# Two-stage kernel (normalised linear attention, then routed experts): outputs stored per pair of tiles, the end of the attention stage reordered, one weight load held back

## The chip, the cores and the metric

The kernel runs on one core of a Trainium2 chip. The metric is the device time of one execution in microseconds. The core has TensorE (PE; PEld is its weight load), VectorE (DVE), ScalarE (ACT), GpSimd (POOL) and SyncE (SP, which only issues DMAs here). ACT, POOL and SP issue DMAs, all of which run on 16 DMA engines.

## What is computed

```python
kv = np.einsum('bhsd,bhse->bhde', k, v)          # 8 batches, 8 heads, 576 rows, 64 columns
out = np.einsum('bhsd,bhde->bhse', q, kv)
rms = np.sqrt(np.mean(out * out, axis=-1, keepdims=True) + 1e-06)
x = out / rms * g_norm                           # -> x: 4608 rows of 512
skip_score = x @ w_skip                          # rows with skip_score <= 0 stay as they are
e_idx = np.argmax(x @ w_gate, axis=1)            # one of 8 experts
gate_w = softmax(x @ w_gate)[e_idx]
h = np.maximum(x @ w1[e], 0.0)                   # 512 -> 1024
x += gate_w * (h @ w2[e])                        # 1024 -> 512, for the rows of expert e
```

All inputs and the output are float32.

## The kernel before, in words

**Attention stage.** The 4608 rows are 36 tiles of 128 rows, taken as 18 pairs. A pair is worked in two units `u`, each for four heads, so there are 36 units, n = 0 to 35. Four batches make a round: each batch has two pairs (`i` = 0, 1) of eight of its nine rows per partition, and a ninth pair (`i is None`, units 16, 17, 34, 35) takes the ninth rows of four batches. The loop at L837 writes the order out by hand. In step n it emits: PE's transposes of q for unit n+1 (`turn`), ACT's root of the sums of squares of unit n-1 (`root`), PE's products of unit n into a PSUM tile and ACT's squares of them (`values`, L466 or L474 and L480), DVE's reciprocal and scaling of unit n-1 (`norm`, L502 and L507, result `xl`), DVE's sum of squares of unit n (`squares`, L488), then PE's work on the state of a later batch, then POOL's adding up of the logits that came along as extra columns (`finish`, L524 to L532, result `lg`). From unit 28 on, three PSUM tiles rotate (two `o_ps` and `sum_ps`, which units 28, 31 and 34 use), so the products of unit n wait for `xl` of unit n-3.

POOL's multiplication by `g_norm` (L547, result `xb`) is put into a list and run one unit later, behind the next reciprocal (`scale`; the note in the code reads "VectorE's port is free then"). `xb` is a buffer for both pairs of a batch, and there are two of them; the ninth pair has one buffer of its own, `x8`. When a buffer is full, the upper 64 partitions are stored by a DMA that POOL issues and the lower 64 by one that SP issues two steps later (L576, L577; L569, L570 for `x8`). Units 34 and 35 are scaled together behind the last logits.

**Choice and ranks.** For three groups of tiles (12, 10 and 14: `ends`), `choose` (L583) turns `lg` into a one-hot choice `ohb` on DVE; `rank` (L614) counts on PE, with an upper triangle `ut` and matrices of ones, each row's place among its expert's rows, and separately the group's count per expert; `number` (L631) adds the sums so far (`top`), picks the place and makes one-hot operands `oha_k`. The first two groups run in pieces inside the loop. After the second, experts are ordered by size, and SP loads expert 0's weights (2 MB `w1`, 2 MB `w2`) into `wpool_a`. `early` places the first 128 rows of the first expert and gathers them from `out`.

**Expert stage** (L867 on). `expert_in` transposes gathered rows on PE (L973) and copies them on ACT (L976, L978); `layer_1` is L996 and L998, `layer_2` is L1007. The stage begins with expert 0's first 128 rows, and the last group is handled between its parts: `choose(LAST)`, `columns` for the first 22 tiles, five eighths of `layer_1`, `rank(LAST)`, `number(LAST)`, the rest of `layer_1`, and `settle` (L680, L743), which places the row numbers in two parts, each beside a part of `layer_2`. Then `slot_rows` and `again_rows` give the row numbers, POOL issues indirect gathers from `out` (L963), which need all stores of x done, and `load_ahead(0)` has SP load expert 1's weights. Experts 1 to 7 use a product scheme with fewer multiplications (L1075 to L1085), whose weight sums DVE makes (L1017, L1023). Results go back by indirect scatters (L1217).

The instructions of each engine stand in the order in which the code emits them; only waits are added.

Of the kernel before, what the change touches and what calls it, by code (L numbers as in the profile page):

```python
# [17 lines left out]
def kernel(  # L18
# [43 lines left out]
    nc = tc.nc  # L62
# [39 lines left out]
    xb_pool = attn.enter_context(tc.tile_pool(name="xb", bufs=2))  # L102
# [43 lines left out]
    room = xb_pool.tile([P, NQ, 2, DM], FP32, tag="xb", name="xb")  # L146
    room = room[:, :, :, :].rearrange("p i r d -> p (i r d)")
# [158 lines left out]
    def load_weights(r, pool):  # L306
        e = experts_of[r]
        w1 = pool.tile([P, DC, F], FP32, tag="w1", name="w1")
        nc.sync.dma_start(out=w1[:, :, :],
                          in_=moe_w1[bass.ds(e, 1)].rearrange("o (c p) f -> p (o c) f", p=P))  # L310
        w2 = pool.tile([P, FC, DM], FP32, tag="w2", name="w2")
        nc.sync.dma_start(out=w2[:, :, :],
                          in_=moe_w2[bass.ds(e, 1)].rearrange("o (c p) d -> p (o c) d", p=P))
        w_sb[r] = (w1, w2)
# [183 lines left out]
    def norm(n):  # L498
# [4 lines left out]
        if n < NU - 1:  # L503
            scale(n, inverse)
# [8 lines left out]
    def finish(n, xl):  # L513
# [20 lines left out]
        if i is None:  # L534
            if u == 0:
                xbs[b, i] = xb_pool.tile([P, 2, DM], FP32, tag="x8", name="x8", bufs=1)
            xb = xbs[b, i]
        else:
            if i == 0 and u == 0:
                xbs[b, 0] = xb_pool.tile([P, NQ, 2, DM], FP32, tag="xb", name="xb")  # L540
            xb = xbs[b, 0][:, i, :, :]
        store = None
        if u == 1 and i is None:
            store = store_8
        elif u == 1 and i == NQ - 1:
            store = store_4
# [5 lines left out]
                .to_broadcast([P, 2, 2, 2 * D]), op=ALU.mult), store and (lambda: store(b))))  # L552
        if n == NU - 1:
            scale(NU)

    def scale(n, behind=None):

        while late:
            job, store = late.pop(0)
            ins = job()  # L560
            if behind:
                tc.add_manual_dep(ins.ins, behind.ins.name, WAIT, reason="VectorE's port is free then")
            if store:
                at(min(n + 2, NU + 1), "end", store())

    def store_8(b):
        xb = xbs.pop((b, None))
        rows = out.rearrange("(f hf r p c) d -> f hf p r c d", f=NF, hf=2, r=2, c=C)[b]
        nc.gpsimd.dma_start(out=rows[0, :, :, C - 1, :], in_=xb[0:64, :, :])  # L569
        return lambda: nc.sync.dma_start(out=rows[1, :, :, C - 1, :], in_=xb[64:128, :, :])  # L570

    def store_4(b):
        xb = xbs.pop((b, 0))
        rows = out[b * S:(b + 1) * S, :].rearrange("(p c) d -> p c d", c=C)[:, 0:4 * NQ, :]
        rows = rows.rearrange("p (i hf r) d -> hf p i (r d)", hf=2, r=2)
        nc.gpsimd.dma_start(out=rows[0], in_=xb[0:64, :, :, :].rearrange("p i r d -> p i (r d)"))  # L576
        return lambda: nc.sync.dma_start(  # L577
            out=rows[1], in_=xb[64:128, :, :, :].rearrange("p i r d -> p i (r d)"))
# [35 lines left out]
    def rank(g):  # L614
# [3 lines left out]
        rk = g_ps[:, GB:GB + nt * E].rearrange("p (t e) -> p t e", e=E)  # L618
        nc.tensor.matmul(out=rk, lhsT=ut[:, :], rhs=ohb, start=True, stop=False,
                         skip_group_check=True)  # L620
        for t in range(nt - 1):
            nc.tensor.matmul(out=rk[:, t + 1:nt, :], lhsT=ones[:, :],
                             rhs=ohb[:, t, :].unsqueeze(1).to_broadcast([P, nt - 1 - t, E]),
                             start=False, stop=(t == nt - 2), skip_group_check=True)
        cnt = g_ps[:, GB + TG * E:GB + TG * E + E]
# [786 lines left out]
```

## Time and profile before

| | us |
|---|---|
| median of 3 runs (lowest, highest) | 402.73 (402.71, 406.16) |
| the profiled execution's own time | 402.42 |
| its span | 400.7 |
| PE busy in the span | 367.6 |
| DVE busy | 243.4 |
| ACT busy | 143.8 |
| POOL busy | 125.5 |
| first PE instruction of the expert stage (L973) | 124.76 |
| last choice begins (L589) | 131.31 |
| first gather of the row numbers (L963) | 143.41 |
| expert 0's remaining rows enter layer 1 (L996) | 152.19 |
| last scatter issued (L1217) | 394.11 |

All times in rows are microseconds from the span's start. A row of the time order has the start, the duration, engine, line, operation, output and inputs, and in brackets how long the engine had been idle ahead of it and what ended that. The 40 slices are 10 us each; a digit is a busy share in tenths, and PEclk is the clock granted to PE in tenths of the full one. A row of the windows view has, for a stretch, its length, the busy time of PE, PEld, DVE, ACT and POOL with the number of instructions, the granted clock, the DMA share and GB/s.

### The profile page before, as it was taken

The page shows a single profiled execution, that of the slowest core. Times are in us where ns is not written, and L with a number is a line of the kernel's source. Part 1 is how long each engine was busy: PE and PEld are TensorE (multiplying, and loading weights), DVE is VectorE, ACT ScalarE, POOL GpSimd, SP SyncE. Part 2 cuts the span into 40 slices and gives each one's busy share as a digit, 9 for nine tenths or more (in the row PEclk, how much of TensorE's full clock was granted, in tenths as well). Part 3 has the DMA queues.
Part 4 walks back from the last instruction along what each step waited for, and adds up shares of the span by engine and source line. Part 5 has one row for each costly group of instructions (what it writes and reads, how often), then busy time and mean ns, then how long its engine had stood idle before and what let it go on. Part 6 is the DMA issues. An engine that isn't in the chain of part 4 may idle for free.

```text
span 400.7 us, 9625 instructions
## 1 busy us (share of the span) xinstructions
PE 367.6 (92%) x3849; PEld 319.6 (80%) x3849; DVE 243.4 (61%) x623; ACT 143.8 (36%) x384; POOL 125.5 (31%) x197
## 2 busy tenths in 40 slices
PE   7789999798975978999999999999999999999992
PEld 4678988798964838849978987988988988989981
DVE  2333567477884870466674775766766766868821
ACT  2265786476852302203510440430430430431410
POOL 7013677465666452012303201221221221212001
PEclk9589999899995998999999999999999999999998
DMA  8999899973793992346252651762762752710001
GB/s 296 395 391 389 280 403 406 406 249 104 260 390 131 258 373 65 99 167 220 77 205 62 246 202 55 262 200 79 255 205 81 253 198 78 254 55 36 18 2 49
DMA packets 31287, 81.70 MB, mean 204 GB/s; under 512 B 1850, under 2 KB 1858, under 8 KB 31236
## 3 DMA queue, kind: packets, MB, share of 16 engines
q1 hardware_dynamic: 26688, 66.59, 47.1%
q0 software_dynamic: 4528, 14.41, 10.3%
q8 instruction: 32, 0.52, 0.5%
q14 instruction: 19, 0.16, 0.1%
q10 hardware_dynamic: 20, 0.02, 0.0%
HBM read 66.80 MB, written 14.48 MB: 203 GB/s over the span
## 4 chain that ended last, share of the span: by engine, by line
PE 54%; issue 16%; DMA 13%; DVE 7%; POOL 5%; ACT 3%; ACTq 0%; POOLq 0%; DVEq 0%
PE bank L1075 23%; DMA out_dram<-xg,rows 7%; PE bank L1007 6%; PE o_ps L466 6%; PE sum_ps L350 4%; PE q_ps L430 4%; PE bank L996 3%; DMA xg<-out_dram,src 3%; DMA xg<-out_dram,asrc 2%; POOL xb L547 2%; PE g_ps L364 2%; DVE xl L507 2%; POOL out_dram L1217 1%; PE bank L973 1%; DMA xb<-in_g_norm_dram 1%
## 5 line engine op out<-in xcount | busy, mean ns | idle before, releaser
L1085 ACT COPY p<-bank 128x128 f32<-128x128 f32 (+6 forms) x70 | 20.8, 297 | 104.8 <-PE bank L1075 90.7
L1075 PE MATMUL bank<-xt,w 128*128 128x128 f32 (+5 forms) x336 | 55.4, 288 | 0.2
L1075 PEld LDWEIGHTS bank<-xt,w 128*128 128x128 f32 x336 | 47.0, 190 | 2.0 <-DVE bank L1079 1.0
L1079 DVE TENSOR_TENSOR bank<-bank,p 128x128 f32<-128x128 f32 (+6 forms) x70 | 23.6, 337 | 40.4 <-PE bank L1075 39.0
L547 POOL TENSOR_TENSOR xb<-xl,g_b 128x512 f32<-128x512 f32 x32 | 38.1, 1190 | 30.7 <-DVE rs L502 26.8
L1217 POOL DMA_INDIRECT out_dram<-xg,rows x16 | 16.3, 1016 | 78.3 <-DVE xg L1214 76.8
L466 PE MATMUL o_ps<-kvd,qT 128*128 128x146 f32 x240 | 36.4, 294 | 1.5 <-DVE xl L507 0.9
L1075 PE MATMUL bank<-xs,s 128*128 128x128 f32 (+5 forms) x224 | 36.7, 289 | 0.0
L1007 PE MATMUL bank<-w,ht 128*32 128x128 f32 (+2 forms) x448 | 36.6, 322 | 0.0
L466 PEld LDWEIGHTS o_ps<-kvd,qT 128*128 128x128 f32 x240 | 32.4, 193 | 2.6 <-DVE xl L507 1.4
L963 POOL DMA_INDIRECT xg<-out_dram,src x15 | 16.8, 1119 | 53.1 <-DMA out_dram<-xg,rows 28.1
L1217 POOL DMA_INDIRECT out_dram<-xg,arows x8 | 9.0, 1130 | 75.4 <-DVE xg L1214 75.1
L1075 PEld LDWEIGHTS bank<-xs,s 128*128 128x128 f32 x224 | 31.1, 190 | 1.0 <-ACT p L1085 0.8
L1007 PEld LDWEIGHTS bank<-w,ht 128*32 128x32 f32 (+2 forms) x448 | 20.4, 121 | 13.6 <-issue 10.9
L488 DVE TENSOR_REDUCE rs<-sq 128x8 f32<-128x512 f32 x36 | 24.4, 678 | 10.9 <-ACT sq L480 10.8
L507 DVE TENSOR_TENSOR xl<-o_ps,rs 128x584 f32<-128x584 f32 x33 | 25.3, 767 | 4.0
L1075 PE MATMUL bank<-w,ht 128*128 128x256 f32 x112 | 27.2, 386 | 0.0
L1075 PE MATMUL bank<-t,ht 128*128 128x256 f32 x112 | 27.1, 385 | 0.0
L350 PE MATMUL sum_ps<-v,k 64*64 64x64 f32 x1152 | 25.9, 233 | 0.8 <-DMA v<-in_v_dram 0.8
L350 PEld LDWEIGHTS sum_ps<-v,k 64*64 64x64 f32 x1152 | 22.6, 143 | 3.7 <-issue 1.6
L1075 PE MATMUL bank<-t,hs 128*128 128x256 f32 x112 | 25.3, 379 | 0.0
L996 PE MATMUL bank<-xt,w 128*128 128x128 f32 (+1 forms) x128 | 23.3, 350 | 1.3 <-ACT xt L976 1.0
(201 smaller groups left out, 683.2 us busy)
## 6 DMA issues: line engine op xcount, KB each, us to landing
w<-in_moe_w_dram SPq DMA_DIRECT2D x16, 2048.0 KB, 10.4
q<-in_q_dram SPq DMA_DIRECT2D x8, 1152.0 KB, 9.9
k<-in_k_dram SPq DMA_DIRECT2D x7, 1152.0 KB, 12.8
v<-in_v_dram SPq DMA_DIRECT2D x7, 1152.0 KB, 15.7
out_dram<-xb POOLq DMA_DIRECT2D x8, 512.0 KB, 8.3
out_dram<-xb SPq DMA_DIRECT2D x8, 512.0 KB, 9.9
k<-in_k_dram SPq DMA_DIRECT2D x2, 576.0 KB, 5.1
v<-in_v_dram SPq DMA_DIRECT2D x2, 576.0 KB, 7.3
```

Source lines behind the costliest of these rows:

```text
L350: nc.tensor.matmul(out=sum_ps[w * 64:(w + 1) * 64, a, u, :], lhsT=kt[r, 2 * u + w, c, :], rhs=vt[r, 2 * u + w, c, :], start=(c == 0), stop ...
L466: nc.tensor.matmul(out=ps[:, w, 0:2 * PK].rearrange("p (r k) -> p r k", r=2)[:, :, cols], lhsT=qT[:, w, a, :], rhs=kvds[b % KVD][:, u, w, ...
L488: nc.vector.tensor_reduce(out=rs[:, :, :], in_=sq[:, :, :, :].rearrange("p x y (a d) -> p x (y a) d", a=2), axis=AX.X, op=ALU.add)
L507: nc.vector.tensor_tensor(out=xl[:, :, :, :].rearrange("p x y (a k) -> p x (y a) k", a=2), in0=ps[:, :, 0:2 * PK].rearrange("p x (h k) -> ...
L547: late.append((lambda: nc.gpsimd.tensor_tensor(out=xb[:, :, 4 * u * D:(4 * u + 4) * D].rearrange("p r (w x) -> p r w x", w=2), in0=xl[:, : ...
L963: nc.gpsimd.indirect_dma_start(out=x_of(xg, off, m), out_offset=None, in_=cut_rows(m)[:, :], in_offset=bass.IndirectOffsetOnAxis(ap=idx[:, ...
L996: nc.tensor.matmul(out=hps[:, cols], lhsT=w_sb[r][0][:, dc, f * P:(f + 1) * P], rhs=xt[:, dc, cols], start=(dc == 0), stop=(dc == DC - 1))
L1007: nc.tensor.matmul(out=yps[q * m:(q + 1) * m, 0:n], lhsT=ht[:, f, off:off + m], rhs=w_sb[r][1][:, f, q * n:(q + 1) * n], start=(f == 0), s ...
L1075: nc.tensor.matmul(out=out, lhsT=lhsT(i), rhs=rhs(i), start=start and i == 0, stop=i == k - 1, skip_group_check=True)
L1079: nc.vector.tensor_tensor(out=to, in0=x, in1=y, op=ALU.add)
L1085: nc.scalar.copy(out=t, in_=x)
L1217: ins = nc.gpsimd.indirect_dma_start(out=cut_rows(m)[:, :], out_offset=bass.IndirectOffsetOnAxis(ap=rows[:, col:col + 1], axis=0), in_=x, ...
```

## The change

- `xb` becomes one buffer per pair, six of them; `x8` is gone. A first pair (`i` = 0) is stored whole by POOL's queue as soon as its second unit is scaled, a second pair whole by SP's queue two steps later, and a ninth pair in halves as before. The staging room for the small parameters at the start moves from `xb` to the space of expert 0's `w2`.
- From unit 30 (`THIRD + 2`) on, `squares(n)` is emitted ahead of `norm(n - 1)`.
- Unit 34 is scaled behind the last reciprocal, as other units are; unit 35 only behind the `columns` of the first 22 tiles. `choose(LAST)` and these `columns` are emitted at the end of the attention loop, and no longer behind the first `expert_in`.
- `rank` begins with an fp32 product of the identity and `top`, one column group wider, so that places and the new sums so far come out of one accumulation; the separate count is gone. `number` loses the two additions and gains a copy. For the last group, `oha_k` is made in two instructions instead of seven.
- The load of expert 1's `w1` (and, behind it on SP's queue, `w2`) waits for the last transposes of expert 0's gathered rows.

```diff
-    xb_pool = attn.enter_context(tc.tile_pool(name="xb", bufs=2))
+    xb_pool = attn.enter_context(tc.tile_pool(name="xb", bufs=6))
...
-    room = xb_pool.tile([P, NQ, 2, DM], FP32, tag="xb", name="xb")
-    room = room[:, :, :, :].rearrange("p i r d -> p (i r d)")
+    room = wpool_a.tile([P, FC, DM], FP32, tag="w2", name="w2")
+    room = room[:, :, :].rearrange("p c d -> p (c d)")
...
-    def load_weights(r, pool):
+    def load_weights(r, pool, behind=None):
...
-        nc.sync.dma_start(out=w1[:, :, :],
+        ins = nc.sync.dma_start(out=w1[:, :, :],
                           in_=moe_w1[bass.ds(e, 1)].rearrange("o (c p) f -> p (o c) f", p=P))
+        if behind:
+            tc.add_manual_dep(ins.ins, behind.ins.name, WAIT, reason="gathers first")
...
         inverse = nc.vector.reciprocal(out=rs[:, :, :], in_=rs[:, :, :])
-        if n < NU - 1:
-            scale(n, inverse)
+        scale(n, inverse)
...
-        if i is None:
-            if u == 0:
-                xbs[b, i] = xb_pool.tile([P, 2, DM], FP32, tag="x8", name="x8", bufs=1)
-            xb = xbs[b, i]
-        else:
-            if i == 0 and u == 0:
-                xbs[b, 0] = xb_pool.tile([P, NQ, 2, DM], FP32, tag="xb", name="xb")
-            xb = xbs[b, 0][:, i, :, :]
...
+        if u == 0:
+            xbs[nq] = xb_pool.tile([P, 2, DM], FP32, tag="xb", name="xb")
+        xb = xbs[nq]
...
-        if n == NU - 1:
-            scale(NU)
...
+    def store_x(nq, b, i):
+
+        xb = xbs.pop(nq)
+        if i is None:
+            rows = out.rearrange("(f hf r p c) d -> f hf p r c d", f=NF, hf=2, r=2, c=C)[b]
+            nc.gpsimd.dma_start(out=rows[0, :, :, C - 1, :], in_=xb[0:64, :, :])
+            return lambda: nc.sync.dma_start(out=rows[1, :, :, C - 1, :], in_=xb[64:128, :, :])
+        rows = out[b * S:(b + 1) * S, :].rearrange("(p c) d -> p c d", c=C)[:, 4 * i:4 * i + 4, :]
+        rows = rows.rearrange("p (hf r) d -> hf p (r d)", hf=2)
+        x = xb[:, :, :].rearrange("p r d -> p (r d)")
+        if i == 0:
+            nc.gpsimd.dma_start(out=rows, in_=x)
+            return None
+        return lambda: nc.sync.dma_start(out=rows, in_=x)
...
-        rk = g_ps[:, GB:GB + nt * E].rearrange("p (t e) -> p t e", e=E)
-        nc.tensor.matmul(out=rk, lhsT=ut[:, :], rhs=ohb, start=True, stop=False,
+        rk = g_ps[:, GB:GB + (nt + 1) * E].rearrange("p (t e) -> p t e", e=E)
+        nc.tensor.matmul(out=rk, lhsT=ident[:, :],
+                         rhs=top[:, :].unsqueeze(1).to_broadcast([P, nt + 1, E]), start=True,
+                         stop=False, skip_group_check=True)
+        nc.tensor.matmul(out=rk[:, 0:nt, :], lhsT=ut[:, :], rhs=ohb, start=False, stop=False,
                          skip_group_check=True)
...
-        nc.vector.tensor_tensor(out=pr, in0=rk, in1=top[:, :].unsqueeze(1).to_broadcast([P, nt, E]),
-                                op=ALU.add)
-        nc.vector.tensor_tensor(out=top[:, :], in0=cnt, in1=top[:, :], op=ALU.add)
-        yield
-        nc.vector.tensor_tensor(out=pr, in0=pr, in1=ohb, op=ALU.mult)
+        nc.vector.tensor_tensor(out=pr, in0=rk[:, 0:nt, :], in1=ohb, op=ALU.mult)
+        nc.vector.tensor_copy(out=top[:, :], in_=rk[:, nt, :])
...
-        for t in range(0, nt, 2):
+        step = 2 if g < LAST else nt // 2
+        for t in range(0, nt, step):
...
+        if THIRD + 2 <= n < NU:
+            squares(n)
         done = norm(n - 1) if 1 <= n <= NU else None
-        if n < NU:
+        if n < THIRD + 2:
             squares(n)
...
+        if n == NU:
+            drain(choose(LAST))
+            first_bv = columns(0, NE, colid_i, row_k, 2, gat_pool, NE)
+            scale(NU, counted[-1])
...
         expert_in(xg0, xt0, first)
-        drain(choose(LAST))
-        bv = columns(0, NE, colid_i, row_k, 2, gat_pool, NE)
         layer_1(0, xt0, ht0, slice(0, P), range(0, 5))
...
-        load_ahead(0)
         gates()
         for piece in plan[0]:
-            expert_in(xg0, xt0, piece)
+            landed = expert_in(xg0, xt0, piece)
+        load_ahead(0, landed)
```

## The prediction

> **What bounds the kernel now.** I read the page first: 40 slices, then the chain. TensorE (PE) is 92% busy, so time is lost only where PE stops or runs at half clock. The slices put both between 110 and 160 us, the seam between attention and experts.
>
> ```profile
> span 400.7 us, 9625 instructions
> ...
> PE 367.6 (92%) x3849; PEld 319.6 (80%) x3849; DVE 243.4 (61%) x623; ACT 143.8 (36%) x384; POOL 125.5 (31%) x197
> ...
> PE   7789999798975978999999999999999999999992
> ...
> PEclk9589999899995998999999999999999999999998
> ```
>
> Then PE's own rows in time order for 117 to 153 us; the bracket is PE's idle time ahead of a row and what ended it.
>
> ```profile
> 120.12 0.74 PE L474 MATMUL o_ps<-kvd,q 64*64 64x73 f32 x32 [1.41 <-DVE xl L507]
> 124.76 1.09 PE L973 MATMUL bank<-ident,xg 128*128 128x128 f32 x4 [3.89 <-DVE xl L507]
> 126.82 6.89 PE L996 MATMUL bank<-xt,w 128*128 128x128 f32 x40 [0.97 <-ACT xt L976]
> 134.60 0.21 PE L619 MATMUL g_ps<-ohb,ut 128*128 128x112 bf16 x1 [0.89 <-DVE ohb L609]
> ...
> 141.75 0.51 PE L680 MATMUL g_ps<-bv,oha_k 128*128 128x48 bf16 x14 [0.21 <-DVE srow L743]
> ...
> 149.59 0.66 PE L973 MATMUL bank<-ident,xg 128*128 128x128 f32 x4 [2.28 <-DMA xg<-out_dram,src]
> 151.12 0.70 PE L973 MATMUL bank<-ident,xg 128*128 128x128 f32 x3 [0.87 <-DMA xg<-out_dram,asrc]
> ```
>
> So PE waits first for the last `xl` tiles, then for `ohb` (the choice of expert for the last 14 tiles), then for gathered rows. GpSimd (POOL) rows say why `ohb` is late, and SyncE's (SP) rows what runs beside the gathers:
>
> ```profile
> 122.68 1.17 POOL L547 TENSOR_TENSOR xb<-xl,g_b 128x512 f32<-128x512 f32 x1 [3.62 <-DVE rs L488]
> ...
> 131.05 0.23 POOL L532 TENSOR_TENSOR lg<-lp 128x18 f32<-128x18 f32 x1
> ```
>
> ```profile
> 106.45 23.38 SPq L577 DMA_DIRECT2D out_dram<-xb  x3
> 133.62 0.59 SPq L570 DMA_DIRECT2D out_dram<-x  x1
> 134.41 0.52 SPq L309 DMA_DIRECT2D w<-in_moe_w_dram  x1
> 135.21 0.54 SPq L312 DMA_DIRECT2D w<-in_moe_w_dram  x1
> ```
>
> The 3.62 us is put down to VectorE (DVE), which had long been done. The instruction opens the buffer of batch 7, one of two, and so waits for both stores of batch 5, one of which stands on SP's queue behind 4 MB of weights issued at 104.5. Last, windows laid on the steps of the granted clock (columns: PE, PEld, DVE, ACT, POOL busy; clock; DMA share; GB/s):
>
> ```profile
> 117.77:121.18 3.41, 1.61 (x66) 1.21 (x64) 2.50 (x6) 1.36 (x4) 0.96 (x3) 1.00 1.04 411
> 121.18:124.59 3.41, 0.00 (x0) 0.00 (x0) 2.26 (x5) 0.99 (x3) 1.75 (x4) 0.50 0.76 264
> ...
> 145.06:148.47 3.41, 2.26 (x6) 0.71 (x4) 3.10 (x14) 0.00 (x0) 2.50 (x3) 1.00 1.04 392
> 148.47:151.89 3.42, 1.36 (x7) 0.76 (x7) 2.27 (x3) 0.88 (x3) 2.81 (x3) 1.00 0.69 229
> 151.89:155.30 3.41, 3.11 (x9) 2.99 (x10) 0.00 (x0) 0.24 (x2) 1.30 (x2) 0.50 0.40 121
> ```
>
> Windows with PE busy 1.61 and 1.36 us are each followed by one at half clock; 2.26 us is not. At 145 to 148 us the DMA share is 1.04: expert 1's weights share the engines with the gathers that PE waits for.
>
> **The change, part by part.** Times are this execution's: span 400.7, run 402.42 us, 0.3 below the median 402.73 of three runs. Units are numbered 0 to 35.
>
> *Six buffers, a store per pair of tiles.* A buffer now comes back after six pairs, so POOL's 3.62 us stall goes, and with it VectorE's 0.69 us wait on POOL before the next-to-last `xl`. That `xl` would follow its reciprocal by 0.34 us, as its neighbours do: 123.34 instead of 123.89, -0.55. Stores are as many and as large; the first halves leave about 10 us earlier, into a DMA share of 1.05. Bounds: nothing, up to one 0.5 MB store at 391 GB/s, 1.3 us of late loads. I take nothing: PE waited for a k or v load once, 0.8 us, before any store.
>
> *Sums of squares a unit ahead (units 30 to 35).* Before, each unit passes through sum, root, reciprocal, `xl` in turn: reciprocals at 118.87, 120.94, 123.00, 2.06 apart. After, the root lies beside the next sum, and VectorE's own starts remain: 0.68 (`xl`) + 0.60 (sum) + 0.33 (reciprocal) = 1.6 to 1.75. But VectorE is in order: unit 30's reciprocal (114.52) now stands behind sum 31, whose squares ScalarE ends at about 115.15 (115.57 before, less 0.4, as the early placement's operand no longer waits for a sum), so it comes at 115.8. Four units on: 122.4 to 122.8; I take 122.75 against 123.00, -0.25. PE's first transposes, which need unit 34's `xl`, move from 124.76 to 123.95 (-0.8); bounds -1.3 to +0.5, should each sum wait for its squares.
>
> *The last choice before the last scaling.* POOL from 117.7 (behind reciprocal 31): five scalings at 1.14, three logit groups at 1.03, two single adds at 0.25, a store of 0.95, together 10.3: `lg` at 128.0 instead of 131.28. The choice took 3.25 us (131.31 to 134.56) because two rows ran beside POOL's scalings, 0.940 and 1.139 us; the like rows of 96 columns took 0.258 and 0.249. So 1.6 us, `ohb` at 129.7. PE gets there at 132.9 (123.95 plus the 8.95 us that it took from 124.76 to 133.71), so the 0.89 us wait goes, with 3 us to spare. The moved columns (0.63 + 1.26) fill VectorE's idle time, and no longer stand before `number`. POOL's last scaling now waits for them: 131.7 to 132.9, store at 133.2 instead of 133.89.
>
> *Ranks that count on.* Each of three ranks loses nt-1 or so bf16 matmuls and gains an fp32 one. The last took 0.81 us; 12 small ones cost 0.30 (72.37 to 72.67), the new one at most as an L364 pair, 0.28: -0.15. VectorE loses 0.27 and about 0.3 (seven rows of 0.35 become two), on no path now: last placement operand at 138.1, PE there at 139.6, so the 0.21 us wait goes too. The other two ranks I count at nothing: PE waits for `xl` later anyway.
>
> Sum up to the end of layer 2's first piece: 0.8 + 0.89 + 0.21 + 0.15 = 2.1, PE done at 145.2 instead of 147.31.
>
> *Expert 1's weights behind the gathers.* Row numbers come 2.1 earlier: gathers issued at 141.3, 143.25, 144.5 (before 143.41, 145.36, 146.66). Landing: 6.2 and 5.7 us beside the weights; without them 3.4 to 3.7 (L963 of 291.35, 351.43) and 2.8 (262.88). So 145.0, 146.1, 147.4, and L996 0.70 behind the last, as before (151.49 to 152.19): 148.1 instead of 152.19, -4.1. If the weights did no harm, the gain is the 2.1 alone. What queues behind SP's new wait are only later weights. Weights are issued at about 148; median landing 10.4, so `w1` by 159, and its first reader (169.02) moves to 163.2, the second half's (183.56) to 177.8: hidden with 4 and 10 us; past that VectorE's sums, then PE's next expert at 182, start late.
>
> *Clock.* PE's idle time between 145.2 and 148.1 falls from 3.5 to 1.7 us. If the clock stays full, layer 1 takes twice 5.82 instead of 7.52 + 5.82: -1.7. The rows bracket it: 1.61 busy of 3.41 was followed by half clock, 2.26 not; here it is 1.7 to 3, depending on where a window begins. I take the clock as kept: most placements leave over 2 us. (The Trainium skill, "TensorE: Matmul & The Clock Gate", Part 1, has the clock fall only after at least one idle window of about 3.4 us. By that rule it stays full, 396.9; by the row with 1.61 us busy, which is no idle window and lost the clock, it can fall, 398.6. The row decides.)
>
> Nothing after 152 us changes: PE-bound, the order stays. Sum: 4.1 + 1.7 = 5.8; 402.73 - 5.8 = 396.9 us (this execution: 396.6).
>
> **Rivals.**
> 1. Clock falls in the shorter gap: 402.73 - 4.1 = 398.6. For: the 1.61 row. Against: little idle.
> 2. Gain paid back by code loading. PE stood 2.15 us for "issue" at 72.20, at DMA share 1.03, and lost the clock for the next window (about 1.6). Expert 1's 4 MB now fall at 148 to 160, beside PE's layer 1, where DMA was almost idle. One such stop: 396.9 + 3.75 = 400.7. Against: only two such stops over 1 us show.
> 3. The change doesn't do it: POOL, with five scalings queued, stays the bound, `lg` stays at 131.3 and gathers are slow for another reason: 401 to 402.7.
> 4. Slower: the gathers wait for the last store, now held behind the columns. Issued at 133.2, it must land by 141.3. Before, it landed by 143.1, within 9.5 us, weights beside it; an `xb` store took 16.1. With 16.1 the gather starts at 149.6, 6.2 later than before; less 2.5 for faster gathers, 406.4. It decides once landing passes 147. Against: no weights compete then.
>
> **How the numbers follow.** Forecast 0.45, rival 1 0.27, rival 2 0.12, rival 3 0.09, rival 4 and other late loads 0.07. Within 1% is about what a measurement of this kernel can tell from no change: 398.7 to 406.8. Forecast and half of rival 1, with a little of the rest, are faster: 0.60; same 0.34, slower 0.06. Low end 394.0: a kept clock also at 128 us (-1.7) and the 1.3 bound at the first transposes. High end 401.6: rivals 1 and 2 and part of 3.
>
> **What would show it.** Right: no POOL row waiting over 1 us before the scaling (L538 there); first transposes near 124; no PE wait before the last rank; gather rows landing in under 4 us; layer 1 from about 148 at clock 1.00; SP's weight row at about 148. Wrong: transposes at or after 124.7 (squares), rank still waiting (POOL), gathers over 5 us, a half-clock window at 148 to 152, an "issue" wait on PE at 148 to 161.

## The result

The changed kernel takes 446.65 us (median of 6 runs, 444.29 to 448.29); the kernel before, on the same chip, 402.98 us (6 runs). The ratio is 1.107, with a 95% interval from 1.101 to 1.112: it is 10.7% slower. The forecast was 396.9 us in a range up to 401.6, with 0.06 for slower. It was wrong in sign and size.

The page of the changed kernel first (448.29 us, span 446.5), with the lines that answer to those of before, and the DMA lines that now matter:

```profile
span 446.5 us, 9564 instructions
...
PE 379.6 (85%) x3822; PEld 329.1 (74%) x3822; DVE 240.6 (54%) x615; ACT 143.9 (32%) x384; POOL 126.6 (28%) x197
...
PE   8789996847279276499999999999999999989992
...
PEclk9999996859579859589999999999999999999998
...
GB/s 310 394 391 318 220 257 245 269 187 185 240 63 325 206 120 75 43 172 350 173 204 140 122 220 91 172 242 182 82 233 230 112 177 189 193 94 2 47 3 45
DMA packets 38344, 81.73 MB, mean 183 GB/s; under 512 B 8906, under 2 KB 8914, under 8 KB 38292
...
q1 hardware_dynamic: 26576, 66.59, 42.3%
q0 software_dynamic: 11696, 14.44, 10.4%
```

PE's busy share falls from 92 to 85%, and the holes in its row of slices (11.2 us each) stand from 67 to 190 us, not at the seam alone. The granted clock is low in nine slices between 67 and 201 us. The lines of the kernel before that answer to these (its slices are 10 us):

```profile
GB/s 296 395 391 389 280 403 406 406 249 104 260 390 131 258 373 65 99 167 220 77 205 62 246 202 55 262 200 79 255 205 81 253 198 78 254 55 36 18 2 49
DMA packets 31287, 81.70 MB, mean 204 GB/s; under 512 B 1850, under 2 KB 1858, under 8 KB 31236
...
q1 hardware_dynamic: 26688, 66.59, 47.1%
q0 software_dynamic: 4528, 14.41, 10.3%
```

From 45 to 112 us the slices of the changed kernel show 185 to 269 GB/s, where the kernel before had 403 to 406 from 50 to 80 us: the transfers of attention arrive more slowly, with the same bytes to move. And one number has changed that no step of the prediction touched: packets under 512 B were 1850 before and are 8906 now. The software queue q0 (GpSimd's) grew from 4528 to 11696 packets, 7168 more, while its bytes stayed at 14.4 MB; q1 (SyncE's) lost 112. Eight pair stores stand on each queue, so a store brought 896 more packets on q0 and 14 fewer on q1. In the packet records the difference lies in packets of 4 bytes alone.

SyncE's issue rows (start, duration) say where the time begins to go:

```profile
43.40 0.71 SPq L568 DMA_DIRECT2D out_dram<-xb  x1
44.16 8.01 SPq L115 DMA_DIRECT2D k<-in_k_dram  x1
52.22 4.93 SPq L115 DMA_DIRECT2D v<-in_v_dram  x1
57.26 6.51 SPq L115 DMA_DIRECT2D q<-in_q_dram  x1
...
66.62 5.60 SPq L115 DMA_DIRECT2D k<-in_k_dram  x1
```

Before, the k rows that answer to these were short:

```profile
43.54 0.61 SPq L115 DMA_DIRECT2D k<-in_k_dram  x1
...
54.41 0.59 SPq L115 DMA_DIRECT2D k<-in_k_dram  x1
...
65.32 0.37 SPq L115 DMA_DIRECT2D k<-in_k_dram  x1
```

Its q rows took 0.37 us, its v rows 1.3 to 3.4. Here the first store of the second pair goes out at 43.40, and from then on nearly every load behind it holds SyncE for 5 to 8 us. PE's rows show who waits:

```profile
73.08 1.56 PE L352 MATMUL sum_ps<-v,k 64*64 64x64 f32 x48 [3.80 <-DMA v<-in_v_dram]
...
93.67 1.56 PE L352 MATMUL sum_ps<-v,k 64*64 64x64 f32 x48 [5.58 <-DMA v<-in_v_dram]
...
112.90 1.56 PE L352 MATMUL sum_ps<-v,k 64*64 64x64 f32 x48 [3.44 <-DMA v<-in_v_dram]
...
125.69 1.09 PE L432 MATMUL q_ps<-ident,q 128*128 128x128 f32 x4 [10.12 <-DMA q<-in_q_dram]
...
158.84 1.09 PE L968 MATMUL bank<-ident,xg 128*128 128x128 f32 x4 [7.66 <-DMA xg<-out_dram,src]
...
184.54 0.72 PE L669 MATMUL g_ps<-bv,oha_k 128*128 128x48 bf16 x14 [9.67 <-DVE srow L732]
```

The batches' v comes late three times, the last q by 10.12 us, the early gather (which reads what the stores wrote) by 7.66. Summed over the trace, PE's waits for v rise from 0.8 to 12.8 us, for q from nothing to 11.6, for gathered rows by way of `src` from 4.0 to 11.5, for `srow` from 0.2 to 9.7: 40.6 us more. PE's busy time grows by 12.0 us (367.6 to 379.6) at the lower clock. That is 52.6; the span grew by 45.8, and the 6.8 between are waits of before that went, the largest 3.9 us for `xl` and 3.4 for "issue".

The 9.7 us at 184.54 are put down to VectorE, and VectorE's own row says nothing more:

```profile
182.78 0.51 DVE L656 TENSOR_TENSOR ohc<-colid_i,hi_k 128x336 bf16<-128x336 int32 x1 [10.97 <-issue]
```

"issue" is a wait that the profile cannot name. The packet records can: SyncE's last pair store has its last data at 182.4 us and its second completion write at 182.6, and the row starts some 0.2 us after that write. Its tile is the first of a pool that opens where attention's pools were. So this wait is most likely a late store as well; that was read off the times, not tried.

**Theory.** It is the order of the dimensions, not the number of bytes. A store of the kernel before was 64 x 2 x 1024 (64 partitions, two pairs, 1024 elements); a store of the changed kernel is 2 x 64 x 1024 in DRAM, because `(hf r)` is split and `hf` put first. If a DMA is spread over as many engines as its outermost dimension allows, the new store runs on 2 of 16 engines. One completion write for each engine used would give 14 fewer packets of 4 bytes a store on SyncE's queue, and that is what q1 lost. **Rival A:** the stores leave at other moments and collide with the loads. **Rival B:** the moved choice, squares, ranks or the held weights cost it.

### The profile page after: what moved, and what is told of

Its sections match the earlier page's. It is cut to its first block, busy times and chain, and to the rows that moved or that the text cites. A ratio compares the mean times of both kernels' runs of the same rounds, so it can differ in the third digit from the quotient of the medians.

```text
span 446.5 us, 9564 instructions
## 1 busy us (share of the span) xinstructions
PE 379.6 (85%) x3822; PEld 329.1 (74%) x3822; DVE 240.6 (54%) x615; ACT 143.9 (32%) x384; POOL 126.6 (28%) x197
## 2 busy tenths in 40 slices
DMA packets 38344, 81.73 MB, mean 183 GB/s; under 512 B 8906, under 2 KB 8914, under 8 KB 38292
## 3 DMA queue, kind: packets, MB, share of 16 engines
q0 software_dynamic: 11696, 14.44, 10.4%
## 4 chain that ended last, share of the span: by engine, by line
PE 48%; DMA 26%; issue 16%; POOL 4%; DVE 3%; ACT 2%; POOLq 1%; ACTq 0%; DVEq 0%
PE bank L1071 22%; DMA q<-in_q_dram 13%; PE bank L1003 8%; DMA out_dram<-xg,rows 5%; PE o_ps L468 4%; DMA out_dram<-xb 3%; PE q_ps L432 3%; PE bank L992 3%; DMA xg<-out_dram,src 2%; PE sum_ps L352 2%; POOL xb L538 2%; PE bank L968 1%; PE g_ps L366 1%; POOL out_dram L1213 1%; DMA w<-in_g_norm_dram 1%
## 5 line engine op out<-in xcount | busy, mean ns | idle before, releaser
L538 POOL TENSOR_TENSOR xb<-xl,g_b 128x512 f32<-128x512 f32 x36 | 42.8, 1189 | 60.5 <-DVE rs L504 56.7
L468 PE MATMUL o_ps<-kvd,qT 128*128 128x146 f32 x240 | 38.7, 306 | 2.5 <-DVE xl L508 2.0
L1003 PE MATMUL bank<-w,ht 128*32 128x128 f32 (+2 forms) x448 | 40.4, 331 | 0.0
L352 PE MATMUL sum_ps<-v,k 64*64 64x64 f32 x1152 | 29.2, 254 | 12.8 <-DMA v<-in_v_dram 12.8
L352 PEld LDWEIGHTS sum_ps<-v,k 64*64 64x64 f32 x1152 | 26.1, 163 | 16.1 <-issue 14.5
L468 PEld LDWEIGHTS o_ps<-kvd,qT 128*128 128x128 f32 x240 | 34.4, 203 | 3.8 <-ACT sq L482 1.6
L432 PE MATMUL q_ps<-ident,q 128*128 128x128 f32 x128 | 23.1, 309 | 11.7 <-DMA q<-in_q_dram 11.6
L1003 PEld LDWEIGHTS bank<-w,ht 128*32 128x32 f32 (+2 forms) x448 | 21.7, 124 | 15.3 <-issue 12.5
L435 ACT COPY qT<-q_ps 128x512 f32<-128x512 f32 x32 | 18.7, 585 | 42.1 <-PE q_ps L432 41.6
L504 DVE RECIPROCAL rs<-rs 128x8 f32<-128x8 f32 x36 | 7.2, 199 | 42.7 <-ACT rs L497 42.6
## 6 DMA issues: line engine op xcount, KB each, us to landing
out_dram<-xb POOLq DMA_DIRECT2D x8, 512.0 KB, 17.2
```

Source lines behind the costliest of these rows:

```text
L352: nc.tensor.matmul(out=sum_ps[w * 64:(w + 1) * 64, a, u, :], lhsT=kt[r, 2 * u + w, c, :], rhs=vt[r, 2 * u + w, c, :], start=(c == 0), stop ...
L432: nc.tensor.transpose(out=ps[:, w, :, hf, :], in_=qts[b][:, 2 * u + w, c:c + 2, :], identity=ident[:, :])
L435: nc.scalar.copy(out=qT[:, :, :, :].rearrange("p w a t -> p (w a t)"), in_=ps[:, :, :, :, :].rearrange("p w a h t -> p (w a h t)"))
L468: nc.tensor.matmul(out=ps[:, w, 0:2 * PK].rearrange("p (r k) -> p r k", r=2)[:, :, cols], lhsT=qT[:, w, a, :], rhs=kvds[b % KVD][:, u, w, ...
L538: late.append((lambda: nc.gpsimd.tensor_tensor(out=xb[:, :, 4 * u * D:(4 * u + 4) * D].rearrange("p r (w x) -> p r w x", w=2), in0=xl[:, : ...
L1003: nc.tensor.matmul(out=yps[q * m:(q + 1) * m, 0:n], lhsT=ht[:, f, off:off + m], rhs=w_sb[r][1][:, f, q * n:(q + 1) * n], start=(f == 0), s ...
```

## The experiments

Times of before beside them were 402.02 to 404.78 us (medians); each ratio is against the runs of before made together with the kernel.

**1 to 3. The pattern cut, on both queues and on each.** The edit in both places (run 2 has it on SyncE's queue only, run 3 on GpSimd's only):

```diff
-            nc.gpsimd.dma_start(out=rows, in_=x)
+            for hf in range(2):
+                nc.gpsimd.dma_start(out=rows[hf], in_=x[hf * 64:(hf + 1) * 64, :])
...
-        return lambda: nc.sync.dma_start(out=rows, in_=x)
+        def lower():
+            for hf in range(2):
+                nc.sync.dma_start(out=rows[hf], in_=x[hf * 64:(hf + 1) * 64, :])
+        return lower
```

> The changed kernel with each store of a pair of tiles cut into two DMAs of 64 partitions (pattern 64x1024 instead of 2x64x1024), on the same queue, at the same place, with the same bytes. Theory (the pattern of the store, whose outermost dimension is 2, puts all of a store's 128 packets on two of the 16 DMA engines; the loads of k, v and q behind it stand in the same line): the whole loss of 43.9 us goes, and the prediction's own steps become visible, so 394 to 402 us; 4-byte packets under 512 B fall from 8906 back to about 1850 to 2000; the SP rows of k, v and q are back at 0.4 to 0.6 us. Rival A (the stores leave at other moments and meet the loads): moments and bytes stay, so 440 to 448 us. Rival B (the moved choice, squares, ranks or the held weights cost it): stays at 440 to 448 us.

Measured: 397.31 us (4 runs), ratio 0.983 (0.973 to 0.994). The whole loss is gone with the same bytes, queues and moments. The page of this kernel and its SyncE rows:

```profile
span 395.0 us, 9589 instructions
...
PE   7689999799966989999999999999999999989992
...
PEclk9699999999996999999999999999999999989998
...
DMA packets 31543, 81.70 MB, mean 207 GB/s; under 512 B 2106, under 2 KB 2114, under 8 KB 31492
```

```profile
42.42 1.19 SPq L571 DMA_DIRECT2D out_dram<-xb  x2
43.65 0.72 SPq L115 DMA_DIRECT2D k<-in_k_dram  x1
...
54.66 0.58 SPq L115 DMA_DIRECT2D k<-in_k_dram  x1
```

2106 packets under 512 B, as before but for the 16 completion writes of each of 16 more stores; k's rows are at 0.72 and 0.58 us. Rivals A and B are out: neither a moment nor a moved operation was changed back.

> The changed kernel with only the stores on SyncE's queue cut into two DMAs of 64x1024; GpSimd's eight keep 2x64x1024. Theory, first form (it is the line on SyncE's queue that the loads stand in): most of the loss goes, 398 to 410 us. Second form (two busy engines delay every transfer that has a share on them, whichever queue sent it): about half stays, 415 to 430 us. Rivals A and B: 440 to 448 us.

Measured: 409.70 us, ratio 1.017 (1.007 to 1.026).

> The mirror of the run before: GpSimd's stores cut into 64x1024, SyncE's eight left at 2x64x1024. Theory, first form: most of the loss stays, 430 to 446 us. Second form: about half, 415 to 430 us. Rivals A and B: 440 to 448 us.

Measured: 444.32 us, ratio 1.100 (1.091 to 1.110). The first form of the theory fits both: the pattern costs 47 us on SyncE's queue (444.3 against 397.3) and 12 us on GpSimd's (409.7). Together they cost 49, so the second adds little to the first. What the 12 us are, the row of the first transposes shows in run 2:

```profile
121.39 0.74 PE L476 MATMUL o_ps<-kvd,q 64*64 64x73 f32 x32 [1.45 <-DVE xl L508]
133.44 1.09 PE L971 MATMUL bank<-ident,xg 128*128 128x128 f32 x4 [11.31 <-DMA xg<-out_dram,src]
```

No load is late there by over 0.8 us; the early gather is, by 11.31 us, since the stores that it reads land 20.4 us behind their issue (median of the page's list of DMA issues; 6.4 us for GpSimd's in run 1).

**4. The pattern alone, in the kernel before.**

```diff
-        rows = rows.rearrange("p (i hf r) d -> hf p i (r d)", hf=2, r=2)
-        nc.gpsimd.dma_start(out=rows[0], in_=xb[0:64, :, :, :].rearrange("p i r d -> p i (r d)"))
+        rows = [rows[:, 4 * i:4 * i + 4, :].rearrange("p (hf r) d -> hf p (r d)", hf=2)
+                for i in range(NQ)]
+        nc.gpsimd.dma_start(out=rows[0], in_=xb[:, 0, :, :].rearrange("p r d -> p (r d)"))
         return lambda: nc.sync.dma_start(
-            out=rows[1], in_=xb[64:128, :, :, :].rearrange("p i r d -> p i (r d)"))
+            out=rows[1], in_=xb[:, 1, :, :].rearrange("p r d -> p (r d)"))
```

> The kernel before, with nothing of the change but the pattern: its two stores per batch each take one pair of tiles over all 128 partitions (2x64x1024) instead of two pairs over 64 (64x2x1024). Same bytes, same two queues, same moments, the two buffers as before. Theory: slower by 20 to 50 us, 423 to 455 us, with packets under 512 B rising from 1850 towards 8900 and SP's load rows at several us. Rivals A and B: 401 to 406 us, as before.

Measured: 452.20 us, ratio 1.119 (1.108 to 1.131), with 8906 packets under 512 B, to the packet as in the changed kernel. With two buffers the loss travels another way: GpSimd waits 51.9 us for `xb` buffers in all, 14.3 at once. The pattern is enough to make the loss, and (run 1) its absence is enough to undo it.

**5. Each transfer by itself.** A kernel that computes nothing of the reference: one store of 512 KB at a time, with 64, 8, 4 and 2 outermost, on either queue.

```python
rows = out[512 * at:512 * at + 512, :].rearrange("(c g p r) d -> c g p (r d)", c=c, g=2, r=2)[:, 0]
```

> Nothing of the reference is computed: after each wait for everything before it, one transfer of the kernel at a time. First eight stores of 512 KB of SBUF, one by one, with 64, 8, 4 and 2 as the outermost dimension of the pattern in DRAM, on SyncE's queue and then on GpSimd's; then a load of k (1152 KB) alone; then that load together with one store of either pattern on either queue, and behind three stores on its own queue. Theory (as many engines as the outermost dimension has, up to 16): from issue to landing a store takes about 3 to 4 us with 64, twice the transfer time with 8, four times with 4, and some 10 to 13 us with 2 (64 packets of 4096 B on each of two engines at the 159 ns that a packet took in the changed kernel are 10.2 us); on GpSimd's queue the same. The load alone lands in 5 to 7 us, behind one store of pattern 64 1 to 2 us later, behind one of pattern 2 some 10 us later, behind three of them some 30 us later. Rival (the pattern is harmless by itself, it was the contention): all eight stores land within 1 us of one another.

Counted from its packet records (us; "in flight" is the packets' summed time over the time from first to last):

```
queue  outermost  issue to landing  data from first to last  in flight  4-byte packets
SyncE     64            3.46                 1.42               14.4           16
SyncE      8            6.26                 4.30                7.2            8
SyncE      4           10.40                 8.52                3.5            4
SyncE      2           13.12                11.29                2.0            2
GpSimd    64            3.47                 1.44               14.3           16
GpSimd     8            6.31                 4.46                7.0          144
GpSimd     4           10.55                 8.54                3.5          400
GpSimd     2           13.80                11.64                2.0          912
```

The engines at work, read from the packets in flight and from the completion writes on SyncE's queue, are as many as the outermost dimension, up to 16: 16, 8, 4, 2. The time grows faster than expected: not twice and four times the 1.42 us with 8 and 4, but three and six times. On GpSimd's queue 64 more packets of 4 bytes come for each engine left out (14 x 64 = 896), which is the changed kernel's surplus. The Trainium skill, "DMA: Bandwidth & Descriptors", section "Why a DMA increments its semaphore by 16 and not by 1", states the rule: the engines are the largest number up to 16 that divides the slowest dimension (other than 1) of both patterns. These rows agree with it. The loads in this run did not stand behind the stores as meant (they went out ahead of them), so they are read from run 13.

**6. The weights not held.** From here on the kernel of run 1 is the base.

```diff
-        gates()
-        for piece in plan[0]:
-            landed = expert_in(xg0, xt0, piece)
-        load_ahead(0, landed)
+        load_ahead(0)
+        gates()
+        for piece in plan[0]:
+            expert_in(xg0, xt0, piece)
```

> The changed kernel with its pair stores cut in two (as in the first run), without the last part of the change: expert 1's weights are asked for ahead of the gates again and wait for nothing. Theory (the prediction's step): the gathers share the engines with 4 MB of weights, land 2.5 to 3.5 us later, and PE's first row of the rest of layer 1 comes at 147 to 148 instead of 144.45: 399.5 to 401 us against 397.3. Rival (the weights do no harm, only the earlier row numbers count): within 0.5 us of the first run's row, 397 us.

Measured: 401.03 us (12 runs), ratio 0.995 (0.992 to 0.999).

```profile
119.44 0.74 PE L476 MATMUL o_ps<-kvd,q 64*64 64x73 f32 x32 [1.44 <-DVE xl L508]
...
145.58 0.83 PE L972 MATMUL bank<-ident,xg 128*128 128x128 f32 x4 [2.19 <-DMA xg<-out_dram,src]
...
149.34 7.67 PE L996 MATMUL bank<-xt,w 128*128 128x212 f32 x32 [0.36 <-ACT xt L977]
```

The theory holds: a gather is waited for 2.19 us again, layer 1 comes 29.90 us behind the last matmul group of attention (119.44) instead of 26.31, and its first half takes 7.67 us, at half clock for a time. Of the 3.59 us, 0.61 lie ahead of the ranks: the stretch at half clock lay later against PE's work (122.04 to 128.87 us, 119.45 to 126.28 in run 1), and the first 40 matmuls of layer 1 up to the ranks took 6.64 us instead of 6.03. The 2.98 behind the ranks are what the hold is worth there.

**7. The choice and the last scaling in their old place.**

```diff
-        if n == NU:
-            drain(choose(LAST))
-            first_bv = columns(0, NE, colid_i, row_k, 2, gat_pool, NE)
-            scale(NU, counted[-1])
...
         expert_in(xg0, xt0, first)
+        drain(choose(LAST))
+        first_bv = columns(0, NE, colid_i, row_k, 2, gat_pool, NE)
```

> The changed kernel with its pair stores cut in two, with the choice for the last 14 tiles back behind the first transposes' copies and the last scaling and the columns where they were. Theory (POOL's logits are out at 126 in either order, and PE has the 40 matmuls of layer 1 to do until 129.2): the choice takes 3.2 instead of 1.6 us, so the ranks' operand comes at about 129.7, PE waits 0 to 0.5 us, and the operands of the last placement come 1 to 2 us later on VectorE: 0.5 to 2 us more than the first run, 398 to 399.5. Rival (the place of the choice is what carries the gain): 401 us or more.

Measured: 397.44 us (6 runs), ratio 0.988 (0.983 to 0.994): no different from the base. Layer 1 comes 26.81 us behind the last matmul group, 0.5 later, all of it in the part at half clock ahead of the ranks (6.52 us instead of 6.03), and PE has no wait ahead of them. The rival is out, and the 0.5 to 2 us that were expected did not come either.

**8. The squares in their old order** (`if n < NU: squares(n)` behind `norm(n - 1)` for all units).

> The changed kernel with its pair stores cut in two, but the sums of squares of units 30 to 35 back behind the reciprocal and scaling of the unit before. Theory (the prediction's step): reciprocals again 2.06 us apart instead of 1.6 to 1.75, so PE's first transposes stand 4.0 to 4.7 us behind the start of its last matmul group of attention instead of 3.28: 0.8 to 1.4 us more than the run that keeps everything. Rival (the sums wait for their squares anyway): 3.3 us, no difference.

Measured: 396.30 us (6 runs), ratio 0.984 (0.980 to 0.988). The time does not tell it from the base; the rows do: reciprocals 2.06 us apart again, the first transposes 4.08 us behind the last matmul group instead of 3.28.

**9. The stores and buffers of before, all else of the change kept** (`bufs=2`, `store_4` and `store_8` as they were).

> The changed kernel with only its first part undone: the stores of the kernel before (two per batch, over 64 partitions, from two buffers), and all else of the change kept. Theory (the prediction's step): POOL again stands some 3 us for a buffer near 120, the logits of the last tiles and with them ranks and gathers come 1 to 3 us later: 398.5 to 400.5 us. Rival (the buffers bring nothing, the rest carries the gain): 396.5 to 398 us, and no row of POOL in the trace that waits over 1 us before a scaling after 110.

Measured: 399.67 us (12 runs), ratio 0.993 (0.989 to 0.996).

```profile
120.21 0.74 PE L476 MATMUL o_ps<-kvd,q 64*64 64x73 f32 x32 [1.44 <-DVE xl L508]
...
132.39 0.21 PE L620 MATMUL g_ps<-ohb,ut 128*128 128x112 bf16 x1 [0.78 <-DVE ohb L607]
...
148.07 7.68 PE L1000 MATMUL bank<-xt,w 128*128 128x212 f32 x32 [0.35 <-ACT xt L981]
```

PE waits 0.78 us for `ohb` again, and layer 1 comes 27.86 us behind the last group, 1.55 later, with its first half at 7.68 us. GpSimd's waits are two, of 1.74 us ahead of 113 and 1.55 ahead of 121, not one of 3.6; the direction is as expected.

**10. All sixteen stores on GpSimd's queue**, pattern 2 x 64 x 1024 kept (`nc.sync.dma_start` becomes `nc.gpsimd.dma_start` in the second pair's store).

> The changed kernel as it is (pattern 2x64x1024 kept), with SyncE's eight pair stores given to GpSimd's queue too. Theory (two engines per store, and a queue serves its transfers in line): the rows of k, v and q on SyncE's queue are back under 2 us and PE no longer waits for them; but 16 stores at the 11.3 us that the transfer of one took by itself are 181 us in one line, from 36 us on, so the last lands near 217 us, and the gathers of expert 0, which read what the stores wrote, come some 70 to 80 us late: 465 to 485 us. Rival (it is the loads' own moment or the contention for all engines): as the changed kernel, 440 to 450 us.

Measured: 416.24 us (2 runs), ratio 1.034 (1.028 to 1.040). Half of this expectation failed. SyncE's load rows are short again, as expected (k, v and q between 0.37 and 2.77 us), PE waits for a load only once, 1.7 us for q, and the rival is out; but the sixteen stores did not make one line of 181 us.

```profile
140.14 1.09 PE L968 MATMUL bank<-ident,xg 128*128 128x128 f32 x4 [15.11 <-DMA xg<-out_dram,src]
```

They land 21.4 us behind their issue (median), and the early gather is late by 15.11 us, not by 70. In the stretch from 60 to 90 us the packet records have 3.8 to 5.2 of the queue's packets in flight, more than the 2.0 of a store on two engines in run 5.

**11. The ranks of before** (`rank` and the start of `number` as they were).

> The changed kernel with its pair stores cut in two, and the ranks of the kernel before (sums for the start added on VectorE). Theory (the prediction's step): 0.15 us on PE and, with the choice early, up to 0.6 us of VectorE behind the ranks: nothing to 0.7 us more, not told apart from the run that keeps everything. Rival (the ranks carry a gain of their own): 2 us or more.

Measured: 396.75 us (6 runs), ratio 0.986 (0.981 to 0.990): not told apart from the base. In the rows layer 1 comes 27.21 us behind the last group, 0.9 later; but 0.80 of it lie ahead of the ranks, in the first part of layer 1 (6.83 us instead of 6.03, with half clock from 124.72 to 131.54), and only 0.10 behind.

**12. The kernel of run 1 again, beside runs 8, 10 and 11.**

> The first run's kernel again (all of the change, pair stores cut in two), beside the kernel before in five rounds and beside the two that each leave a part out. Expected from the first run: 395 to 399 us, 1.0 to 2.5% under the kernel before, with PE's first row of the rest of layer 1 at 144 to 147 us.

Measured: 398.03 us (6 runs), ratio 0.988 (0.984 to 0.993); layer 1 starts at 145.81, which is 26.38 us behind the last group. This is the version that beats both kernels, the one before by 1.2%: the change with its pair stores cut in two. Runs 7, 8 and 11, each without one part, are as fast (396.30 to 397.44 us). So in the time only the held weights show (run 6 is 3.0 to 3.7 us above runs 12 and 1) and, less clearly, the buffers (run 9 is 1.6 to 2.4 above, with an interval that overlaps run 12's).

**13. Trains of stores with a load behind them.** Run 10 left open why a queue matters. Nothing of the reference is computed here either.

```python
for stores in ((), (sp_64,), (sp_2,), (pool_64,), (pool_2,), (sp_64,) * 3, (sp_2,) * 3,
               (pool_64,) * 3, (pool_2,) * 3):
```

> Nothing of the reference is computed. In each of nine steps everything before has landed; then no store, one, or three of 512 KB are sent on one queue, and some 2 us later one load of k (1152 KB) on SyncE's queue. Theory A (each queue puts all two-engine stores on the same pair): three of pattern 2x64x1024 take some 34 us on either queue (three times 11.3), with 2 packets in flight at a time. Theory B (SyncE's queue uses one pair, GpSimd's goes from pair to pair): three take some 32 to 35 us on SyncE's queue, but 13 to 18 us on GpSimd's, with 4 to 6 packets in flight. Under both, the load alone takes 5.5 to 7 us, some 10 us more behind one store of pattern 2 on its own queue and some 20 to 27 us more behind three; behind those on GpSimd's queue 0 to 3 us more under B (its share of each pair waits for less), and as much as behind SyncE's if the pairs are the same ones. With 64 as the outermost dimension, three take 6 to 9 us and the load 1 to 4 us more, on either queue.

VectorE clears the load's tile just before the load is sent and again once it has landed, so the brackets are the time from the load's issue to its landing, with one exception below. They stand in the order of that list, without the two single stores with 64 outermost (6.06 and 6.16); the two SyncE rows are the sending of three stores with 64 and with 2 outermost:

```profile
15.31 1.98 DVE L38 MEMSET t<- 128x2304 f32 x1 [6.41 <-DMA t<-in_k_dram]
...
48.32 1.98 DVE L38 MEMSET t<- 128x2304 f32 x1 [11.74 <-DMA t<-in_k_dram]
...
82.65 1.98 DVE L38 MEMSET t<- 128x2304 f32 x1 [12.96 <-DMA t<-in_k_dram]
...
85.73 2.69 SPq L58 DMA_DIRECT2D out_dram<-x  x3
...
96.31 1.98 DVE L38 MEMSET t<- 128x2304 f32 x1 [6.05 <-DMA t<-in_k_dram]
...
99.39 9.37 SPq L49 DMA_DIRECT2D out_dram<-x  x3
...
135.63 1.98 DVE L38 MEMSET t<- 128x2304 f32 x1 [31.71 <-DMA t<-in_k_dram]
...
149.60 1.98 DVE L38 MEMSET t<- 128x2304 f32 x1 [6.37 <-DMA t<-in_k_dram]
...
172.86 1.98 DVE L38 MEMSET t<- 128x2304 f32 x1 [15.65 <-DMA t<-in_k_dram]
```

Alone 6.41 us; behind stores with 64 outermost, one or three, on either queue, 6.05 to 6.37. Behind one store with 2 outermost 11.74 (SyncE's queue) and 12.96 (GpSimd's); behind three, 31.71 and 15.65. (The exception is the 31.71: there SyncE was still sending the stores, and the load's own row starts 4.9 us into the wait, at 108.85, and lasts 9.6.)

The packet records give the reason. The queue does not hold a load back as a whole: behind one two-engine store on SyncE's queue, 449 of the load's 512 packets start while the store's data still move, and 448 would be 14 sixteenths of them. Only the share of the two busy engines has to wait. Three stores on SyncE's queue take 31.3 us with 2.04 packets in flight, so all use the same pair; three on GpSimd's take 19.1 us with 4.2 in flight, so they use different ones. That is theory B, but several of its figures were off. The load behind GpSimd's stores took 6.6 and 9.2 us more, not 0 to 3: its last share waits for the busy pair, whoever sent the store. One store on its own queue cost it 5.3 us, not some 10. GpSimd's three took 19.1 us, not 13 to 18; and three with 64 outermost took 4.0 and 4.8 us, not 6 to 9, and cost the load nothing. SyncE itself is held 9.37 us by sending three stores (2.69 with 64 outermost), a row like those of 5 to 8 us in the changed kernel.

## Why the prediction was wrong, point by point

- **The step that failed** is in "Six buffers, a store per pair of tiles": "Stores are as many and as large; the first halves leave about 10 us earlier, into a DMA share of 1.05. Bounds: nothing, up to one 0.5 MB store at 391 GB/s, 1.3 us of late loads. I take nothing". The count and the bytes are right and the rate is not. 391 GB/s is the rate of 16 engines; a store on two took 11.29 us for 512 KB, 46 GB/s. So a store's data move in 11.3 us instead of 1.4, in batches that come 10 to 11 us apart, and the loads on the same queue have a share on that pair: the queue falls behind in every batch. The diff shows the pattern plainly (`hf p (r d)` without an index on `hf`), and the prediction read it for its size only. Its upper bound took the rate for granted, so the range could not hold the case.
- **GpSimd's stall and six buffers:** right. -0.55 us was predicted at the first transposes; from the last matmul group to them it is 4.64 us before and 4.08 in run 8 (new stores, old squares). Together with the squares 0.8 was predicted there, with a bound of 1.3; run 1 has 1.36. Run 9, with two buffers, puts the `ohb` wait back (0.78 us; 0.89 was predicted to go) and 1.55 us on the stage.
- **Squares ahead:** right in kind, too small. -0.25 was predicted; run 8 against run 1 gives 0.80 (4.08 to 3.28).
- **The choice:** its length is right (1.71 us from 126.39 to 128.10 in run 1, predicted 1.6), its worth is not. Run 7 without it has no wait at PE either, and run 9, with it but with the stores and buffers of before, waits 0.78 us: the new stores and buffers removed the 0.89, not the place of the choice.
- **Ranks:** predicted -0.15 us of PE; from the ranks to layer 1's rest it is 15.33 us in run 11 and 15.23 in run 1, so 0.10, not visible in the time.
- **Weights behind the gathers:** right in mechanism, too small. The prediction gave the hold 2.0 of its 4.1 us; run 6 shows 2.98 behind the ranks, and then the clock.

```profile
118.14 0.74 PE L476 MATMUL o_ps<-kvd,q 64*64 64x73 f32 x32 [1.44 <-DVE xl L508]
121.42 1.09 PE L972 MATMUL bank<-ident,xg 128*128 128x128 f32 x4 [2.54 <-DVE rs L504]
...
142.40 0.44 PE L972 MATMUL bank<-ident,xg 128*128 128x128 f32 x2 [0.49 <-DMA xg<-out_dram,asrc]
143.77 0.33 PE L972 MATMUL bank<-ident,xg 128*128 128x128 f32 x1 [0.93 <-DMA xg<-out_dram,asrc]
144.45 6.00 PE L996 MATMUL bank<-xt,w 128*128 128x212 f32 x32 [0.35 <-ACT xt L977]
...
150.87 5.98 PE L996 MATMUL bank<-xt,w 128*128 128x212 f32 x32
```

- These rows of run 1 answer to PE's rows of before in the prediction: from the last matmul group (120.12 before, 118.14 here) to layer 1 it is 32.07 us before and 26.31 here.
- **Clock:** kept, as taken. Layer 1's first half takes 6.00 us (7.52 before), 7.67 and 7.68 in runs 6 and 9. On the steps of run 1's own clock (3.41 us each), the two windows around its start have PE busy 2.42 and 2.63 us, within the 1.7 to 3 that the prediction took:

```profile
139.93:143.35 3.42, 2.42 (x10) 1.08 (x8) 3.15 (x10) 0.96 (x2) 2.51 (x4) 1.00 0.32 98
143.35:146.76 3.41, 2.63 (x14) 2.45 (x15) 1.56 (x2) 0.61 (x2) 2.80 (x3) 1.00 0.71 153
```

In run 6 the window ahead of the fall (142.52 to 145.93) has 1.22 us, in run 9 (145.31 to 148.72) 1.94. But run 1 has one with 1.93 (112.63 to 116.04) that full clock followed, so PE's busy time alone does not decide it; what does stays open.

- **"Nothing after 152 us changes":** not quite. At the last gate product run 1 is 9.3 us ahead (167.39 to 158.13), at the end of the span 5.7. Its PE waits 4.0 us for gathered rows after 160 us, where before had 1.14 in four rows, and the clock falls to 0.80 at 344 to 351 us. That the experts now come sooner upon the scatters that their gathers wait for is likely, but was not tried. Run 12 has the same 4.0 us, run 7 only 1.9.
- **The sum** for all that is not the pattern was -5.8 us, a ratio of 0.986. Runs 1 and 12 gave 0.983 (0.973 to 0.994) and 0.988 (0.984 to 0.993). That the total fits is in part luck: at the last gate product run 1 was 9.3 us ahead and run 12 7.9, more than forecast, and 3.6 to 3.8 us of it went again in the stretch that was put at nothing. The hold, the buffers and the squares went the way that was forecast, with other sizes, and the place of the choice was worth nothing that shows; and the term for the stores, put at nothing, cost 49 us (446.65 against 397.31).
- **Rivals:** the slower one (a last store that lands late) had the right fact, "an `xb` store took 16.1", and took it for an accident at the end; with the new pattern the median of GpSimd's eight stores was 17.2. No rival named the order of the store's dimensions.

## What to carry to other kernels

When a store is cut anew, read its access pattern as well as its bytes: here an outermost dimension of 2 meant two engines, and 512 KB then needed 11.3 us instead of 1.4. Slice such a dimension away with one DMA for each index, as run 1 did. In a profile, look at the durations of the issue rows and at the count of small packets; the count alone is not enough. It betrays such stores on GpSimd's queue (8906 packets under 512 B), but run 3, with them on SyncE's queue only, has 1866, hardly more than the kernel before, and takes 444 us. A queue that carries both stores and the loads that an engine waits for is the worst place for a slow store (47 us against 12 on the other queue), but a store on the other queue delays a load as well (run 13).

## What the runs showed of the hardware

- A store with 2, 4, 8 or 64 as its outermost dimension had 2.0, 3.5, 7.2 and 14.4 packets in flight; transfer took 11.29, 8.52, 4.30 and 1.42 us. Twice the engines did not halve it between 2 and 4: a packet took 0.18 us on average with two engines at work and 0.23 with four. Why is open.
- Run 13's two-engine stores on SyncE's queue all used one pair (31.3 us for three), those on GpSimd's different pairs (19.1 us). A load behind one on SyncE's queue still started 449 of its 512 packets beside it. Which pair a store takes in the whole kernel was not measured.
- Sending is not free: loads of k and q that took SyncE 0.4 to 0.6 us to send took up to 8.5 us behind two-engine stores.
- A two-engine store on GpSimd's queue leaves 912 packets of 4 bytes instead of 16, on SyncE's 2 instead of 16.
